# Two more staging places in attention, and the down weights' split moved to behind the third output part, in a fused attention and MoE kernel

## The chip, the cores and the metric

The kernel runs on one core of one Trainium2 chip. The metric is the device time of one execution in microseconds; lower is better. Three runs of the kernel before gave 858.66, 855.82 and 859.16 us, median 858.66. A separate profiled execution gave the trace from which all rows here come.

## The reference

```python
def reference(**kwargs):
    # kernelised attention, 4 batches x 8 heads x 576 tokens x 64
    proj = einsum('bhsd,df->bhsf', x, w_phi); proj -= max(abs(proj), -1)
    phi = concatenate([exp(proj), exp(-proj)], -1)
    attn = (phi(q) @ (phi(k).T @ v)) / (phi(q) @ sum(phi(k)) + 1e-6)
    x = attn.reshape(2304, 512)
    # dense gated MLP, 512 -> 1536 -> 512
    g = x @ w_gate
    x = (g / (1 + exp(-g)) * (x @ w_val)) @ w_out
    # top-1 mixture, 8 experts, 512 -> 1024 -> 512
    e = argmax(x @ gate); out = prob[e] * sigmoid(x @ output_gate)[e] * relu(x @ w1[e]) @ w2[e]
```

All inputs are fp32 (this is a shortened form; the softmax of the gate and the mask by expert are left out).

## The kernel before, in words

**Attention** takes the span up to about 155 us: 16 units (two heads each), with the order of the instructions of all engines written down in `PLAN_TABLE`. Beside it the MLP's weights are brought into the resident tiles `WR[f][0..2]` (f is one of 12 slices of the hidden width; [0] and [1] are gate and value, [2] is the down weight, called W2 below). Ten of the 36 tiles are brought in later, one to a block, by `conv_late` (L447 and L456 on ACT, L464 and L468 on DVE, L472 on POOL). The transposed attention output of the token blocks behind the first two leaves through a staging place: `x_keep` (ACT, L415) copies a piece of PSUM to `XS[i]`, `x_store` (L419) sends it to DRAM, and the place is free when the transfer has landed. There are two places, `TS` and `GP`.

**The MLP** is computed for three pairs of token blocks, p = 0, 1, 2, of 768 tokens each. Every fp32 operand is split in two fp32r parts, hi and lo: `cut` copies hi on ACT (L551) and subtracts it from the source for lo (L548) on DVE or POOL. A product is then three matmuls, hi*hi, hi*lo, lo*hi (L591 to L593, and L494 to L496). Gate and value are made for both token blocks at once from seven products instead of eight, so that sums of weights (`weight_sum`, four per slice, L560, POOL) and sums of the two halves of the input stand in for plain operands. `pair(p)` runs 12 blocks f. In program order a block issues on PE

A11 (6 matmuls), O0 (3), A12 (6), S2 (6), O1 (3), first half of S3 (3), S1 (6), second half of S3 (3), O2 (3), S4 (6), A22 (6),

where O0, O1, O2 (`o_part`) are the down projection of the slice two blocks back, for three tiles of tokens, with the split W2. Below, s is the start of the last matmul of S1 in a block. The other engines' parts of a block:

- `copy` (L619, ACT) takes PSUM to SBUF: `sp1` behind A11, `su2` behind S2, `su4` behind S1.
- `gate` is a tanh (L622, ACT) and an elementwise operation (L623, DVE) from PSUM.
- `add` (L616, DVE): `add(pa, su4, py)` behind S3, on which A22 waits, since A22 goes on in the bank `py`; `add(hb, gb, pa)` at the end, on which the next block's A12 waits, since it starts in the bank of `pa`.
- three splits for the next block: `pair_split(3f+3)` of a plain weight, lo on POOL, and behind it the four weight sums of a later slice; `pair_split(3f+4)` and `pair_split(3f+5)` of weight sums, lo on DVE. They are called the first, second and third split here. The first two weight sums write over what the second split reads, the other two over what the third reads.
- the split of W2 for the next block's O0 (lo on POOL, 128x512), and `cut22`, the split for A22 (lo on POOL, 128x256).
- one step of `rest`, the small operations of the routing of earlier tokens (L883), in p = 1 and 2.

`down(p)` follows each pair: 12 iterations of 9 matmuls project the kept second halves (`hb`), with their splits issued two iterations ahead, and two more groups of three tiles with W2 at iterations 0 and 2. From iteration 3 on, `fill` pops one entry of a list (`post`: three logits steps with L924 and L925, then L932 and L934, L939 and L940, then routing). In the last `down`, 2 MB weight loads of the first expert run beside it.

What decides the order: in attention the table; behind it Tile's scheduler, by its own estimate, under the data dependences and under `tie`, a dependence of the schedule alone (no semaphore) on the matmul in `state["pe"]`. Each engine then runs its own instructions in that order.

Of the kernel before, what the change touches and what calls it, by code (L numbers as in the profile page):

```python
# [53 lines left out]
class Arena:  # L54
# [10 lines left out]

PLAN_LOG = None
PLAN_TABLE = [
# [34 lines left out]


class Plan:
# [84 lines left out]
def kernel(ctx, tc, qT, kT, v1, wphi, w1cat, wlog, mw1, mw2, consts, out):  # L189
# [80 lines left out]
    assert st + 1664 <= ar.p  # L270
    TS = buf(BT)
    GP = buf(BT)
    XS = [TS, GP]
    offs["KR"] = ar.p
    QK = [buf(2 * S) for _ in range(2)]
    V = [buf(VW) for _ in range(2)]
# [212 lines left out]
    def o_tiles(on, last, ts, out_, g, w):  # L489
        (gh, gl), (woh, wol) = g, w  # L490
        for t in ts:
            ps = PS[:, out_[t], :]
            ts_ = slice(t * P, (t + 1) * P)
            PE.matmul(ps, gh[:, ts_], woh, start=not on, stop=False)  # L494
            PE.matmul(ps, gh[:, ts_], wol, start=False, stop=False)
            mm = PE.matmul(ps, gl[:, ts_], woh, start=False, stop=last)  # L496
        return mm
# [50 lines left out]
        eng.tensor_tensor(out=w[1], in0=src, in1=w[0].bitcast(F32), op=ALU.subtract)  # L548

    def cut(w, src, eng):  # L550
        ACT.activation(w[0], src, AF.Copy)  # L551
        cut_lo(w, src, eng)

    def weight_sum(f, i, eng=None):
# [58 lines left out]
    def pair(p, rest):  # L613

        def add(out_, x, y, op=ALU.add):
            DVE.tensor_tensor(out=out_, in0=x, in1=y, op=op)  # L616
# [17 lines left out]
        def o_part(f, ts):  # L634
            g = f - 2
            if g >= 0:
                o_tiles(g != 0, False, ts, bk["O"], (GH[g % 2], GL[g % 2]), W2)

        for f in range(p == 0, NFT):
            sp1, su2, su4, gb = TMP  # L640
            bb = BB[f % 2]
            pb = PS[:, bb, :BT]
            product(p, f, "A11", bb, True)
            copy(sp1, pb)
            o_part(f, (0,))
            hidden(f - 1)
            product(p, f, "A12", BA, True)
            add(pa, sp1, pa)
            product(p, f, "S2", bb, False)
            copy(su2, pb)  # L650
            gate(GP, pa)
            pair_split(48 * p + 3 * f + 3)
            o_part(f, (1,))
            product(p, f, "S3", BY, True, (0,))
            rest(p, f, 0)
            product(p, f, "S1", bb, False)
            copy(su4, pb)
            if f == NFT - 1:
                cut(g5(p, 0), hb(p, stretch(p)[0]), DVE)
            pair_split(48 * p + 3 * f + 4)  # L660
            product(p, f, "S3", BY, True, (1,))
            add(pa, su4, py)
            o_part(f, (2,))
            rest(p, f, 1)
            product(p, f, "S4", bb, False)
            gate(gb, pb)
            if f == NFT - 1:
                cut(g5(p, 1), hb(p, stretch(p)[1]), DVE)
            pair_split(48 * p + 3 * f + 5)
            product(p, f, "A22", BY, False)  # L670
            add(hb(p, f), gb, pa, ALU.mult)
            if p < NP - 1:
                SP.dma_start(out=hd[p][f], in_=hb(p, f))
            add(py, su2, py)
            add(py, GP, py, ALU.mult)
            cut22(f + 1)
            if f:
                cut(W2, WR[f - 1][2], POOL)
            rest(p, f, 2)
        hidden(NFT - 1)  # L680

    def first_part():
# [13 lines left out]
        def unit(u, d0):  # L696
# [23 lines left out]
            for part in range(2):  # L720
                h = op("PE", 36 - 12 * part, lambda b, part=part: tx_mm(u, part, b), [("xt", 0), ("xt2", 1)] if part == 0 else
                       [("xt2", 0), ("xt", 1)], [("txm", u, part)], 1, due=d0 + 17)
                for x in x_pieces(u, part):
                    j, w = x[1], 17 + x[3] * 8 // 100
                    if j < 2:
                        op("ACT", w, lambda b, x=x: x_copy(u, x, b, ACT), [("txm", u, part)], [("xf", j, u)], holder=h, due=d0 + 17,
                           alt=("DVE", w, lambda b, x=x: x_copy(u, x, b, DVE)))
                        continue
                    i = len(kept) % 2
                    kept.append(x)  # L730
                    op("ACT", w, lambda b, x=x, i=i: x_keep(u, x, b, i), [("txm", u, part)], [("xs", i)], holder=h, due=d0 + 17)
                    op("SP", 30, lambda x=x, i=i: x_store(u, x, i), [("queue",), ("xs", i)], [("xdma", len(kept))], due=d0 + 18)
# [703 lines left out]
    def down(p):  # L1436
# [8 lines left out]
        for i, f in enumerate(order_):  # L1445
# [4 lines left out]
                pair_split(48 * p + 39 + i)  # L1450
            if not end and i + 4 < NFT:
                SP.dma_start(out=HS3[order_[i + 4] % 4], in_=hd[p][order_[i + 4]])
            mm = o_tiles(i > 0, i == NFT - 1, range(3), bk["O2"], g5(p, i), w)
            state["pe"] = mm.ins
            if end and 2 <= i < 6:
                gather_q(0, [i - 2])
            if i == 0:
                o_tiles(True, False, range(3), bk["O"], (GH[0], GL[0]), W2)
                cut(W2, WR[NFT - 1][2], POOL)
            if i == 1 and end:  # L1460
                load_w(0, 1)
# [1 line left out]
            if i == 2:  # L1463
                o_tiles(True, True, range(3), bk["O"], (GH[1], GL[1]), W2)
                for t in range(3):
                    post_x2(n - 1, t)
            if i >= 3 and (end or i < 8):
                fill(1)
            if not end:
                if i >= 3 and xs:  # L1470
# [21 lines left out]
    for i in range(2):  # L1492
        load_w(1, i)
    state["banks"] = [7]
    todo += [(idle, ())] * 3 + post(5) + route_late()
    quads(fill)
    ch = Chunks()
    moe2(NQ, NQ + NSS, ch)
# [51 lines left out]
```

## Time and profile before

| what | value |
|---|---|
| median of three runs | 858.66 us (855.82 to 859.16) |
| profiled execution | 858.48 us, its span 856.7 us |
| granted clock of TensorE, mean | 0.995 |
| busy PE, DVE, ACT, POOL | 97%, 70%, 59%, 52% of the span |
| stages (start, us) | attention 0, block f=0 of p=0 155.6, down 277, p=1 311, down 425, p=2 458, down 574, experts 612.5 |

PE's busy time counts matmuls whose ends are modelled, so 97% says only that it seldom stands still. A row of the timeline has the start, the duration, engine and line, the operation and, in brackets, how long the engine was idle before it and what released it.

### The profile page before, as it was taken

The numbers are of one execution on the slowest core, as the hardware profiler recorded it, in microseconds if no ns is written. First come the engines' busy times: TensorE is split into PE (matmuls) and PEld (weight loads), VectorE is DVE, ScalarE is ACT, GpSimd is POOL, SyncE is SP. The second block draws the span as 40 slices with busy tenths as digits, with TensorE's granted clock in tenths as the row PEclk, the third lists the DMA queues.
The fourth block names the chain that finished last, engine by engine and source line by source line (L and its number), as shares of the span: only waits on it lengthen the run. The fifth ranks groups of instructions, "written<-read, shape, count | busy, mean of one in ns | idle before, by whom it ended". The sixth has DMA issues, their size and how long they took to land. (4 is left out here: it accounts for less than half of the span.)

```text
span 856.7 us, 17319 instructions
## 1 busy us (share of the span) xinstructions
PE 827.2 (97%) x6701; PEld 723.2 (84%) x6701; DVE 595.6 (70%) x1106; ACT 504.9 (59%) x938; POOL 443.9 (52%) x414
## 2 busy tenths in 40 slices
PE   8999999899999999999999999998999999999995
PEld 5999899798889789999978899996778888888884
DVE  6999899777777668666776777774686434445692
ACT  5787888566666566546656565563434434344883
POOL 2877889777677556556655566446202111120120
PEclk9999999999999999999999999999999999999998
DMA  9676784412222230000121000019402331010650
GB/s 253 193 227 169 237 246 153 135 53 79 78 69 71 93 111 28 19 19 20 56 83 37 2 1 1 2 27 388 151 1 63 136 124 73 24 51 0 248 212 11
DMA packets 30875, 84.57 MB, mean 99 GB/s; under 512 B 6462, under 2 KB 15678, under 8 KB 29504
## 3 DMA queue, kind: packets, MB, share of 16 engines
q1 hardware_dynamic: 27216, 73.57, 26.7%
q0 software_dynamic: 3200, 9.48, 3.4%
q8 instruction: 54, 0.88, 0.5%
q10 hardware_dynamic: 368, 0.33, 0.2%
q14 instruction: 37, 0.30, 0.1%
HBM read 79.13 MB, written 17.86 MB: 113 GB/s over the span
## 5 line engine op out<-in xcount | busy, mean ns | idle before, releaser
L551 ACT ACTIVATE r_dense<-arena 128x512 fp32r<-128x512 f32 (+1 forms) x150 | 92.8, 622 | 102.2 <-PE banks L592 70.7
L560 POOL TENSOR_TENSOR arena<-arena 128x256 f32<-128x256 f32 x140 | 103.9, 753 | 90.7 <-DVE r_dense L548 87.6
L548 POOL TENSOR_TENSOR r_dense<-arena,r_dense 128x512 fp32r<-128x512 f32 x73 | 97.7, 1339 | 42.2 <-ACT r_dense L551 36.5
L591 PE MATMUL banks<-arena_r,r_dense 128*128 128x384 f32 x288 | 98.1, 343 | 3.5 <-ACT arena L415 1.9
L1215 ACT ACTIVATE arena_r<-arena 128x512 fp32r<-128x512 f32 x64 | 40.3, 633 | 102.1 <-PE banks L1226 49.2
L548 DVE TENSOR_TENSOR r_dense<-arena,r_dense 128x512 fp32r<-128x512 f32 (+1 forms) x83 | 70.2, 846 | 43.2 <-ACT r_dense L551 20.8
L1218 DVE TENSOR_TENSOR arena_r<-arena,arena_r 128x512 fp32r<-128x512 f32 x64 | 44.4, 694 | 79.7 <-ACT arena_r L1215 78.5
L593 PE MATMUL banks<-arena_r,r_dense 128*128 128x384 f32 x288 | 97.0, 337 | 0.0
L592 PE MATMUL banks<-arena_r,r_dense 128*128 128x384 f32 x288 | 96.8, 336 | 0.0
L616 DVE TENSOR_TENSOR banks<-arena,banks 128x384 f32<-128x384 f32 x140 | 77.8, 556 | 12.6 <-PE banks L593 9.8
L1176 POOL DMA_INDIRECT out_dram<-arena x20 | 24.1, 1204 | 106.1 <-ACT arena L1270 41.0
L1171 POOL DMA_INDIRECT ov_gather<-x2d,arena x20 | 21.0, 1048 | 100.4 <-PE banks L1185 54.8
L591 PEld LDWEIGHTS banks<-arena_r,r_dense 128*128 128x128 f32 x288 | 53.9, 188 | 15.4 <-ACT arena L619 2.7
L619 ACT ACTIVATE arena<-banks 128x384 f32<-128x384 f32 x105 | 50.7, 484 | 25.0 <-PE banks L593 23.2
L623 DVE SCALAR_TENSOR_TENSOR arena<-arena,banks 128x384 f32<-128x384 f32 x70 | 38.7, 553 | 35.1 <-ACT arena L622 34.9
L548 POOL TENSOR_TENSOR arena_r<-arena,arena_r 128x512 fp32r<-128x512 f32 x36 | 47.5, 1321 | 21.5 <-ACT arena_r L551 21.5
L592 PEld LDWEIGHTS banks<-arena_r,r_dense 128*128 128x128 f32 x288 | 54.1, 188 | 2.0
L593 PEld LDWEIGHTS banks<-arena_r,r_dense 128*128 128x128 f32 x288 | 54.1, 188 | 0.1
L332 DVE TENSOR_REDUCE arena<-banks 128x6 f32<-128x768 f32 x48 | 45.8, 955 | 9.5 <-PE banks L326 6.8
L591 PE MATMUL banks<-ov_pair,r_dense 128*128 128x384 f32 x144 | 49.7, 345 | 1.3 <-ACT arena L619 0.9
L1225 PE MATMUL banks<-arena_r 128*128 128x512 f32 x128 | 50.4, 393 | 0.0
L1226 PE MATMUL banks<-arena_r 128*128 128x512 f32 x128 | 49.9, 390 | 0.0
(217 smaller groups left out, 2376.0 us busy)
## 6 DMA issues: line engine op xcount, KB each, us to landing
arena<-mw SPq DMA_DIRECT2D x16, 2048.0 KB, 8.7
ov_conv<-w1cat SPq DMA_DIRECT2D x18, 512.0 KB, 6.1
arena<-w1cat SPq DMA_DIRECT2D x18, 512.0 KB, 3.5
arena<-v SPq DMA_DIRECT2D x16, 325.0 KB, 3.8
hd<-arena SPq DMA_DIRECT2D x24, 192.0 KB, 1.8
x2d<-arena SPq DMA_DIRECT2D x18, 256.0 KB, 3.9
arena<-qT SPq DMA_DIRECT2D x15, 288.0 KB, 4.3
arena<-kT SPq DMA_DIRECT2D x15, 288.0 KB, 6.8
```

Source lines behind the costliest of these rows:

```text
L332: DVE.tensor_reduce(out=MX, in_=ps, axis=AX.X, op=ALU.max, apply_absolute_value=True)
L548: eng.tensor_tensor(out=w[1], in0=src, in1=w[0].bitcast(F32), op=ALU.subtract)
L551: ACT.activation(w[0], src, AF.Copy)
L560: (eng or POOL).tensor_tensor(out=o, in0=x, in1=y, op=op)
L591: PE.matmul(ps, w[0][:, c], xh[:, k, :], start=(start and k == 0), stop=False, skip_group_check=True)
L592: PE.matmul(ps, w[0][:, c], xl[:, k, :], start=False, stop=False, skip_group_check=True)
L593: state["pe"] = PE.matmul(ps, w[1][:, c], xh[:, k, :], start=False, stop=(k == 1), skip_group_check=True).ins
L616: DVE.tensor_tensor(out=out_, in0=x, in1=y, op=op)
L619: ACT.activation(out_, x, AF.Copy)
L1218: DVE.tensor_tensor(out=l, in0=src, in1=h.bitcast(F32), op=ALU.subtract)
L1225: PE.matmul(ps, wh[:, c], XQH[:, k, :], start=(k == 0), stop=False)
L1226: PE.matmul(ps, wh[:, c], XQL[:, k, :], start=False, stop=False)
```

## The change

The change has six parts. (1) `x_keep` has four staging places instead of two; the two new ones are the first 384 columns of the W2 tiles of slices 10 and 11, which are brought in later. (2) The table of attention's order is a new one. (3) The hi copy of every `cut` is tied to the last matmul in `state["pe"]`, which `o_part` now sets too. (4) In a block the second split stands behind the second half of S3 and `add(pa, su4, py)`, no more ahead of them. (5) The split of W2 stands right behind O2, no more at the end of the block. (6) In `down`, iteration 0 computes two tiles of its own, then the three tiles with W2, then its third tile; `fill` runs at iterations 5 to 11 of the last `down` (before 3 to 11), and 4 to 8 of the others (before 3 to 7); and one idle entry of the list is taken out before the last token block's steps.

```diff
 PLAN_TABLE = [
-    0, 2, 4, 5, 6, 1, 3, 14, 15, 16, 531, 538, 29, 17, 18, 21, 532, 30, 31, 7, 19, 43, 45, 47, 22, 32, 10, 20, 33, 539,
+    0, 1, 14, 15, 2, 3, 5, 16, 17, 4, 18, 538, 29, 531, 21, 19, 532, 30, 6, 7, 8, 1534, 31, 539, 32, 43, 22, 45, 44, 20,
...
-    XS = [TS, GP]
+    XS = [TS, GP] + [WR[NFT - 2 + i][2][:, 0:BT] for i in range(2)]
...
     def cut(w, src, eng):
-        ACT.activation(w[0], src, AF.Copy)
+        a = ACT.activation(w[0], src, AF.Copy)
+        if "pe" in state:
+            tie(a)
         cut_lo(w, src, eng)
...
         def o_part(f, ts):
             g = f - 2
             if g >= 0:
-                o_tiles(g != 0, False, ts, bk["O"], (GH[g % 2], GL[g % 2]), W2)
+                state["pe"] = o_tiles(g != 0, False, ts, bk["O"], (GH[g % 2], GL[g % 2]), W2).ins
...
                 cut(g5(p, 0), hb(p, stretch(p)[0]), DVE)
-            pair_split(48 * p + 3 * f + 4)
             product(p, f, "S3", BY, True, (1,))
             add(pa, su4, py)
+            pair_split(48 * p + 3 * f + 4)
             o_part(f, (2,))
+            if f:
+                cut(W2, WR[f - 1][2], POOL)
             rest(p, f, 1)
...
             cut22(f + 1)
-            if f:
-                cut(W2, WR[f - 1][2], POOL)
             rest(p, f, 2)
...
-                    i = len(kept) % 2
+                    i = len(kept) % 4
...
-            mm = o_tiles(i > 0, i == NFT - 1, range(3), bk["O2"], g5(p, i), w)
+            if i == 0:
+                o_tiles(False, False, (0, 1), bk["O2"], g5(p, i), w)
+                o_tiles(True, False, range(3), bk["O"], (GH[0], GL[0]), W2)
+            mm = o_tiles(i > 0, i == NFT - 1, range(3) if i else (2,), bk["O2"], g5(p, i), w)
             state["pe"] = mm.ins
...
             if i == 0:
-                o_tiles(True, False, range(3), bk["O"], (GH[0], GL[0]), W2)
                 cut(W2, WR[NFT - 1][2], POOL)
...
-            if i >= 3 and (end or i < 8):
+            if i >= 5 if end else 4 <= i < 9:
                 fill(1)
...
-    todo += [(idle, ())] * 3 + post(5) + route_late()
+    todo += [(idle, ())] * 2 + post(5) + route_late()
```

On DVE, a middle block of p = 1. L616 to `r_dense` is the lo part of the hidden slice; the L548 are the second and third split; L623 the two gates; of the L616 to `banks`, the second is `add(pa, su4, py)`. Before:

```order
L616 TENSOR_TENSOR r_dense<-banks,r_dense 128x384
L616 TENSOR_TENSOR banks<-arena,banks 128x384
L548 TENSOR_TENSOR r_dense<-arena,r_dense 128x512
L623 SCALAR_TENSOR_TENSOR arena<-arena,banks 128x384
L548 TENSOR_TENSOR r_dense<-arena,r_dense 128x512
L616 TENSOR_TENSOR banks<-arena,banks 128x384
L883 TENSOR_TENSOR arena<-arena,banks 128x24
L623 SCALAR_TENSOR_TENSOR arena<-arena,banks 128x384
L616 TENSOR_TENSOR banks<-arena,banks 128x384
L616 TENSOR_TENSOR arena<-arena,banks 128x384
```

The same block with the change (L616 is now L618, L623 is L625):

```order
L618 TENSOR_TENSOR r_dense<-banks,r_dense 128x384
L618 TENSOR_TENSOR banks<-arena,banks 128x384
L625 SCALAR_TENSOR_TENSOR arena<-arena,banks 128x384
L618 TENSOR_TENSOR banks<-arena,banks 128x384
L548 TENSOR_TENSOR r_dense<-arena,r_dense 128x512 x2
L625 SCALAR_TENSOR_TENSOR arena<-arena,banks 128x384
L618 TENSOR_TENSOR banks<-arena,banks 128x384
L618 TENSOR_TENSOR arena<-arena,banks 128x384
L618 TENSOR_TENSOR banks<-arena,banks 128x384
```

Both splits have moved behind `add(pa, su4, py)`, and stand together ahead of the second gate.

On POOL, a middle block of p = 1: to `arena_r` is the lo part of W2, to `r_dense` that of the first split, to `arena_r_63` that of `cut22`, L560 the weight sums. Before:

```order
L560 TENSOR_TENSOR arena<-arena 128x256 x4
L548 TENSOR_TENSOR arena_r<-arena,arena_r 128x512
L548 TENSOR_TENSOR r_dense<-arena,r_dense 128x512
L548 TENSOR_TENSOR arena_r_63<-arena,ov_pair 128x256
L560 TENSOR_TENSOR arena<-arena 128x256 x4
```

With the change (L560 is now L562):

```order
L548 TENSOR_TENSOR r_dense<-arena,r_dense 128x512
L562 TENSOR_TENSOR arena<-arena 128x256
L548 TENSOR_TENSOR arena_r<-arena,arena_r 128x512
L562 TENSOR_TENSOR arena<-arena 128x256 x3
L548 TENSOR_TENSOR arena_r_63<-arena,ov_pair 128x256
```

The lo part of W2 has moved from behind all four sums to behind the first of them.

On POOL, late blocks of p = 0, where L472 is the last step of `conv_late`. Before:

```order
L560 TENSOR_TENSOR arena<-arena 128x256 x2
L472 TENSOR_TENSOR arena<-arena 128x512
L560 TENSOR_TENSOR arena<-arena 128x256 x2
L548 TENSOR_TENSOR arena_r<-arena,arena_r 128x512
L548 TENSOR_TENSOR r_dense<-arena,r_dense 128x512
L548 TENSOR_TENSOR arena_r_63<-arena,ov_pair 128x256
```

With the change:

```order
L548 TENSOR_TENSOR r_dense<-arena,r_dense 128x512
L472 TENSOR_TENSOR arena<-arena 128x512
L548 TENSOR_TENSOR arena_r<-arena,arena_r 128x512
L562 TENSOR_TENSOR arena<-arena 128x256 x4
L548 TENSOR_TENSOR arena_r_63<-arena,ov_pair 128x256
```

Here L472 and the lo part of W2 now stand next to each other, ahead of all four sums.

## Rows read from the trace of the kernel before

**Rows 1.** The page's busy time by engine: busy us, share of the span, instructions.

```profile
PE 827.2 (97%) x6701; PEld 723.2 (84%) x6701; DVE 595.6 (70%) x1106; ACT 504.9 (59%) x938; POOL 443.9 (52%) x414
```

**Rows 2.** Busy time by stretch (PE, PEld, DVE, ACT, POOL, clock, DMA): the blocks of p = 0 and of p = 1.

```profile
169.50:277.00 107.50, 104.05 (x547) 95.19 (x547) 83.35 (x131) 70.17 (x139) 79.91 (x86) 1.00 0.22 71
...
311.40:425.00 113.60, 112.79 (x631) 105.75 (x630) 76.17 (x165) 67.04 (x139) 71.24 (x81) 1.00 0.12 39
```

**Rows 3.** PE's waits: line, what released it, total us, times, longest us.

```profile
PE banks L591 <- DVE banks L616: 3.2, 8, 0.4
PE banks L924 <- DVE arena L925: 2.4, 1, 2.4
...
PE banks L591 <- ACT arena L415: 1.9, 2, 1.0
PE banks L591 <- ACT arena L619: 1.7, 2, 0.9
...
PE banks L494 <- DVE arena L616: 0.8, 1, 0.8
```

**Rows 4.** Timeline of ACT at the start of p = 0.

```profile
157.94 0.33 ACT L415 ACTIVATE arena<-banks 128x192 f32<-128x192 f32 x1 [2.57 <-DMA xd<-arena]
...
162.72 0.66 ACT L456 ACTIVATE arena<-arena 128x512 int32<-128x512 uint32 x1 [1.39 <-DMA arena<-w1cat]
```

**Rows 5.** Timeline of one block of p = 0: DVE, POOL, then PE.

```profile
203.46 1.57 DVE L548 TENSOR_TENSOR r_dense<-arena,r_dense 128x512 fp32r<-128x512 f32 x1 [0.35 <-PE banks L593]
...
203.18 1.29 POOL L472 TENSOR_TENSOR arena<-arena 128x512 int32<-128x512 int32 x1 [0.71 <-DVE arena L468]
...
205.55 0.44 PE L591 MATMUL banks<-arena_r,ov_pair 128*128 128x384 f32 x1 [0.41 <-DVE banks L616]
```

**Rows 6.** Timeline of one block of p = 1: PE, ACT, DVE, then POOL.

```profile
393.39 0.33 PE L593 MATMUL banks<-ov_pair,r_dense 128*128 128x384 f32 x1
...
394.55 0.40 PE L496 MATMUL banks<-arena_r,r_dense 128*128 128x512 f32 x1
...
398.60 0.34 PE L591 MATMUL banks<-arena_r,r_dense 128*128 128x384 f32 x1
...
394.13 0.47 ACT L619 ACTIVATE arena<-banks 128x384 f32<-128x384 f32 x1
395.04 0.63 ACT L551 ACTIVATE arena_r<-arena 128x512 fp32r<-128x512 f32 x1 [0.44 <-PE banks L496]
...
396.89 0.56 DVE L623 SCALAR_TENSOR_TENSOR arena<-arena,banks 128x384 f32<-128x384 f32 x1 [1.02 <-ACT arena L622]
...
397.83 0.55 DVE L616 TENSOR_TENSOR arena<-arena,banks 128x384 f32<-128x384 f32 x1
...
395.02 1.46 POOL L560 TENSOR_TENSOR arena<-arena 128x256 f32<-128x256 f32 x2 [1.70 <-DVE r_dense L548]
```

**Rows 7.** Timelines of DVE and POOL where both work, at 268 and 326 us.

```profile
269.43 2.16 DVE L548 TENSOR_TENSOR arena_r<-arena,arena_r 128x384 fp32r<-128x384 f32 x2
...
268.86 1.30 POOL L548 TENSOR_TENSOR r_dense<-arena,r_dense 128x512 fp32r<-128x512 f32 x1
270.11 1.05 POOL L548 TENSOR_TENSOR arena_r<-arena,ov_pair 128x256 fp32r<-128x256 f32 x1
...
326.14 0.48 DVE L883 TENSOR_TENSOR arena<-arena 128x24 f32<-128x24 f32 x1
326.54 0.68 DVE L548 TENSOR_TENSOR r_dense<-arena,r_dense 128x512 fp32r<-128x512 f32 x1
...
325.83 3.37 POOL L560 TENSOR_TENSOR arena<-arena 128x256 f32<-128x256 f32 x4 [2.90 <-DVE r_dense L548]
```

**Rows 8.** The last down: timeline of DVE, then busy time of two stretches.

```profile
593.08 0.69 DVE L925 COPY arena<-banks 128x512 f32<-128x512 f32 x1 [1.99 <-DMA x2d<-arena]
...
595.00:597.00 2.00, 2.00 (x10) 1.10 (x12) 0.96 (x2) 0.39 (x1) 0.00 (x0) 0.52 1.06 447
597.00:599.00 2.00, 2.00 (x11) 0.68 (x12) 1.05 (x2) 0.72 (x2) 1.20 (x1) 0.63 1.01 419
```

66 rows, old and new, of the table PLAN_TABLE are left out of this document.

## The prediction

> **What bounds it now.** I read the busy time by engine first: PE 97%, DVE 70%, ACT 59%, POOL 52% [rows 1]. So the kernel is bound by PE, and what a change of order can give back is the time in which PE stands still, or runs at the lower clock. By stretch, PE is idle 3.45 of 107.5 us in p = 0 and only 0.8 of 113.6 us in p = 1 [rows 2]: there is something to win in p = 0, and nearly nothing in p = 1 and p = 2, where the change can only cost. The list of PE's waits names the places [rows 3]: eight waits on an `add` of DVE (3.2 us), one of 2.4 us on the logits' copy L925, two on `x_keep` (1.9), two on the copies L619 (1.7), one of 0.8 us at the start of a `down`. The timelines of these places then give the causes.
>
> **How DVE and POOL get in each other's way.** This decides most of the sum. In p = 0, POOL's L472 ran from 203.18 to 204.47; DVE's split, which takes 0.68 us alone [rows 7], began at 203.46 and ended at 205.03, so 0.56 us behind POOL's end [rows 5]. It did nothing while POOL's operation lasted. Two rules follow, and I price by them: an operation of DVE with two SBUF inputs waits for the end of a POOL operation that was there first, and then needs 0.56 us; and one of DVE that already waits goes ahead of POOL's next. For the second: at 326 us a small DVE operation waited out POOL's first sum, ended at 326.62, and DVE's split ran in 0.68 us directly behind it, while POOL's four sums took 3.37 us [rows 7], where two take 1.46 [rows 6]. At 268.86 the turns alternated: POOL, DVE, POOL (1.05 us for a 128x256 split), DVE, the two DVE splits taking 2.16 us [rows 7].
>
> The Trainium skill (SBUF — State Buffer, section "SBUF: two separate sides") says that the pair of ports which the two share is held for a whole instruction by whichever starts first; the trace agrees on that (0.56 us behind POOL's end, above). It says nothing of who is next when both wait.
>
> **The sum, part by part** (profiled execution 858.48 us, which is its span of 856.7 and 1.8 around it; 0.2 below the median).
>
> *Attention, four places.* ACT stood idle 2.57 us ahead of an `x_keep` until a transfer had landed [rows 4], and PE then waited 1.9 us in two places [rows 3]; each wait also costs a slow restart. With two more places this goes. But the 1.39 us that ACT waited for a load of weights [rows 4] stays, and the order of all of attention is new. Best case 5, worst 0; I take -3.0. The two new places lie in tiles that are brought in late in p = 0, when their stores have long landed, so they cost nothing themselves; SP issues the same transfers.
>
> *p = 0.* The third split now stands behind `add(pa, su4, py)`, so the eight waits ahead of A22 go: 3.2 us and 0.11 each for the restart (0.44 against 0.33 us) [rows 5, 6], together -4.2. In their place: L472 and then the lo part of W2 stand on POOL just when DVE wants both splits. From s (the start of S1's last matmul) L472 ends at about s+2.0 to 2.3. The second split then ends at s+2.6 to 2.9; W2's lo part, 1.15 to 1.29 us like the POOL operations of its shape [rows 5, 7], holds POOL until s+3.8 to 4.1; the third split ends at s+4.3 to 4.6. Behind it stand the gate and the `add` to `hb`. Now the gate starts 3.50 and `hb` ends 4.99 behind s, and the next A12, which waits for `hb`, starts 5.21 behind s [rows 6]: 0.2 us to spare, and the gate 0.8 to 1.1 late. That is a new wait of 0.6 to 0.9 ahead of A12; 0.8 in nine blocks is +7.2. Together **+3.0** (0 to +5).
>
> *The ties* are no semaphores, so they cost only through the order that results, which is priced here by block.
>
> *p = 1 and 2, the clean block.* `su4` can start at about s+0.4 and takes 0.47 [rows 6]; activations overlap by 0.1; the second split's hi, 0.63, ends at s+1.4 and its lo part at s+2.1. POOL's first sum waits for that and takes 0.73 (half of 1.46): it ends at about s+2.93. W2's hi part follows O2's last matmul by 0.49, at s+1.65 [rows 6], and the third split's hi by the tie behind it: it ends at s+2.80. The lo part of the third split asks at s+2.83, so 0.1 us before the sum ends. By the second rule it goes ahead of W2's lo part, ends at s+3.6, and `hb` at s+5.1: no wait. W2's lo part then ends at s+4.8 to 4.9, where O0 needs it about half a us ahead of A12, so at s+4.74: 0.08 in some 18 blocks, +1.5.
>
> *p = 1 and 2, blocks in which DVE is late.* In f = 1 of both, the lo part of W2 stands ahead of all sums: +0.4 each, +0.8. In five more the third split cannot ask before s+2.93: two have an exp of the routing ahead of its hi part on ACT, one has two logits copies of 0.69 [rows 8] ahead of it on DVE, one a reciprocal behind a small operation that had to wait, one a 128x384 product. There W2's lo part goes first, 1.15 to 1.29, and `hb` is late by some 1.05: **+5.2**. In five others a small operation with two SBUF inputs waits out the sum directly ahead of the split; as at 326 us it costs nothing, as at 268 us 1.1: half, +2.7. Both waits on L619 were there before [rows 3]; the earlier `su4` takes some of them: -1.0.
>
> *Downs.* The 0.8 us wait [rows 3] and its restart go, since the tiles with W2 now stand ahead of the third tile: -1.0. In the last one PE waited 2.4 us for L925 [rows 3], which waited for the store of x2 to land, behind the 2 MB loads (DVE at 593.08) [rows 8]. Two iterations later the store has landed: -2.5, and 0.3 for a smaller wait behind it. PE also fell to the lower clock after standing still, 0.52 of full speed in 595 to 597 and 0.63 in 597 to 599 [rows 8]; 48% and 37% of 2 us are 1.7 us: -1.7. The steps that no longer fit go into the experts' start: +0.5. Together **-5.0** (-7 to 0).
>
> -3.0 + 3.0 + 1.5 + 0.8 + 5.2 + 2.7 - 1.0 - 5.0 = +4.2. Laid on the median of 858.66, which is 0.2 above the profiled execution, that is 862.9: **863 us**. 0.5%, about what a measurement of this kernel can tell from no change, is 4.3 us, so this lies at the edge of slower.
>
> **Rivals.**
>
> *The port is no trouble (faster).* If DVE also gets its turn where I have it lose, and L472 in p = 0 is done earlier, the +5.2, +2.7, +1.5 and half of the +7.2 go: 863 - 13 = 850 us. For it: at 326 us DVE kept the port over two operations. Against it: 203.46. It is decided by whether the third split asks before the first sum ends.
>
> *DVE loses in every block (slower).* The margin in the clean block is 0.1 us out of sums of eight durations. If POOL's next operation takes the port at the sum's end, `hb` is 1.0 late in another 13 blocks or so: 863 + 13 = 876 us. For it: POOL's instructions follow each other without a gap. Against it: 326.54. By the page's words the pair is free between two instructions of POOL, which speaks for DVE's turn; no rule there gives it to POOL.
>
> *The last down keeps its wait.* The loads go on beyond 599 us at a full DMA share, 1.06 and 1.01 [rows 8], so a later logits step may meet them too, and PE's waits stay in attention because of the load of weights: 863 + 4 = 867 us.
>
> **How the numbers follow.** My forecast 0.45, spread around the bound (0.25 slower, 0.15 within 0.5%, and 0.05 faster, if attention gives its full 5 and the unsure collisions nothing); port no trouble 0.30 (0.25 faster, 0.05 within); DVE always late 0.12; the last down keeps its wait 0.13 (0.10 slower, 0.03 within). So faster 0.30, same 0.23, slower 0.47. The forecast's own range is 855 to 869; with the rivals, leaving out a tenth on each side, 848 to 877.
>
> **What will show it.** Right: no waits of PE on L618 ahead of A22 in p = 0, but waits ahead of A12 there on L618 to `hb`, of 0.5 to 0.9 us in most blocks; in p = 1 and 2 such waits of about 1 us in five to ten blocks and none in the clean ones; no wait on the logits' copy and a full clock in the last down; `x_keep` not held by its store. Wrong: waits ahead of A12 in nearly all blocks (the second rival) or nearly none (the first), or PE still idle in attention's last 10 us.

## The result, and the profile after

The changed kernel took 866.27 us (median of four runs, 866.07 to 867.5) against 857.52 for the kernel before in the same comparison (four runs, 855.82 to 859.16): ratio 1.0105, 95% interval 1.008 to 1.0131, so about 1% slower. The profiled execution's span grew from 856.7 to 865.7 us. The prediction was 863, slower, with a range of 848 to 877.

The page's busy time by engine, after:

```profile
PE 829.9 (96%) x6701; PEld 725.2 (84%) x6702; DVE 621.4 (72%) x1103; ACT 498.1 (58%) x937; POOL 467.8 (54%) x418
```

PE does the same 6701 matmuls in nearly the same time. DVE is busy 25.8 us longer than in [rows 1], with three instructions fewer, and POOL 23.9 us longer, with four more. Those four are operations of attention, some 8 us of work; most of the rest is none, since an operation that waits for the other engine counts as busy. DVE's splits show it, before and after (the second number behind the bar is the mean in ns):

```profile
L548 DVE TENSOR_TENSOR r_dense<-arena,r_dense 128x512 fp32r<-128x512 f32 x71 | 59.0, 832 | 31.5 <-PE banks L593 20.6 <-ACT r_dense L551 9.1 <-ACT r_dense L794 1.8
L548 DVE TENSOR_TENSOR r_dense<-arena,r_dense 128x512 fp32r<-128x512 f32 x72 | 80.3, 1119 | 10.2 <-ACT r_dense L551 10.0
```

The list of PE's waits, after (line, what released it, total us, times, longest us; L593 to L595 are the product's matmuls, L618 is `add`, L832 and L835 are the same steps of ACT and DVE in block 0):

```profile
PE banks L593 <- DVE arena L618: 11.8, 19, 0.8
PE banks L593 <- DVE banks L835: 1.7, 1, 1.7
...
PE banks L593 <- ACT arena L621: 1.2, 2, 0.6
...
PE banks L387 <- issue: 1.1, 1, 1.1
PE banks L593 <- ACT arena L832: 0.9, 1, 0.9
PE banks L357 <- issue: 0.9, 2, 0.7
...
PE banks L495 <- POOL arena_r L548: 0.2, 1, 0.2
```

Against [rows 3], the eight waits of 3.2 us ahead of A22 (`add` to `banks`) are gone, and so are those on L925 and on `x_keep` in the blocks. In their place stand nineteen waits of 11.8 us on `add` to `arena`: that is `hb`, on which A12 waits. In block 0 of p = 0 the wait on L835 grew from 0.3 to 1.7 us, that on L832 from 0.4 to 0.9.

Where the time went, from the start of the first matmul of each stage:

| stage | before, us | after, us | difference |
|---|---|---|---|
| attention, to block 0 of p = 0 | 155.59 | 158.48 | +2.89 |
| p = 0, blocks 0 and 1 | 21.96 | 21.06 | -0.90 |
| p = 0, blocks 2 to 10 | 90.28 | 92.35 | +2.07 |
| block 11 and the first down | 43.58 | 42.80 | -0.78 |
| p = 1, block 0 | 8.81 | 9.60 | +0.79 |
| p = 1, blocks 1 to 10 | 95.50 | 100.55 | +5.05 |
| block 11 and the second down | 42.67 | 41.75 | -0.92 |
| p = 2, blocks 0 to 10 | 105.56 | 109.27 | +3.71 |
| block 11, the last down, the experts | 292.75 | 289.84 | -2.91 |

Timeline of one block of p = 0 after (compare [rows 5]): DVE, POOL, PE.

```profile
207.88 3.14 DVE L548 TENSOR_TENSOR r_dense<-arena,r_dense 128x512 fp32r<-128x512 f32 x2
210.94 0.54 DVE L625 SCALAR_TENSOR_TENSOR arena<-arena,banks 128x384 f32<-128x384 f32 x1
...
211.87 0.54 DVE L618 TENSOR_TENSOR arena<-arena,banks 128x384 f32<-128x384 f32 x1
...
207.47 1.30 POOL L472 TENSOR_TENSOR arena<-arena 128x512 int32<-128x512 int32 x1 [2.04 <-DVE arena L468]
208.81 1.66 POOL L548 TENSOR_TENSOR arena_r<-arena,arena_r 128x512 fp32r<-128x512 f32 x1
...
212.47 0.44 PE L593 MATMUL banks<-arena_r,r_dense 128*128 128x384 f32 x1 [0.63 <-DVE arena L618]
```

The chain that was forecast can be read off. POOL's L472 ends at 208.77; DVE's second split waited for it. W2's lo part then holds POOL until 210.47, and the third split, the second of the two in the first row, ends at 211.02, 0.55 behind it. The gate follows at 210.94, `hb` ends at 212.41, and A12 starts at 212.47 after 0.63 us of nothing.

Two blocks of p = 1 after, first one without a wait, then one with:

```profile
350.67 0.69 DVE L548 TENSOR_TENSOR r_dense<-arena,r_dense 128x512 fp32r<-128x512 f32 x1 [0.45 <-ACT r_dense L551]
...
350.02 0.74 POOL L562 TENSOR_TENSOR arena<-arena 128x256 f32<-128x256 f32 x1 [2.98 <-DVE arena L885]
350.72 1.80 POOL L548 TENSOR_TENSOR arena_r<-arena,arena_r 128x512 fp32r<-128x512 f32 x1
```

```profile
392.02 0.83 DVE L885 TENSOR_TENSOR arena<-arena 128x24 f32<-128x24 f32 x2
392.78 1.78 DVE L548 TENSOR_TENSOR r_dense<-arena,r_dense 128x512 fp32r<-128x512 f32 x1
...
391.98 0.74 POOL L562 TENSOR_TENSOR arena<-arena 128x256 f32<-128x256 f32 x1 [2.79 <-DVE r_dense L548]
392.68 1.33 POOL L548 TENSOR_TENSOR arena_r<-arena,arena_r 128x512 fp32r<-128x512 f32 x1
...
396.00 0.45 PE L593 MATMUL banks<-arena_r,r_dense 128*128 128x384 f32 x1 [0.82 <-DVE arena L618]
```

In the first, the third split asks at 350.67, while the sum runs to 350.76, and goes next; W2's lo part takes 1.80 in place of 1.30, since it waits. In the second, two small operations of the routing waited out the sum, the split came 0.1 us behind POOL's next, and took 1.78.

### The profile page after: what moved, and what is told of

The parts are those of the page before. It is cut to its first block, busy times and chain, and to the rows that moved or that the text cites. A ratio compares the mean times of both kernels' runs of the same rounds, so it can differ in the third digit from the quotient of the medians.

```text
span 865.7 us, 17185 instructions
## 1 busy us (share of the span) xinstructions
PE 829.9 (96%) x6701; PEld 725.2 (84%) x6702; DVE 621.4 (72%) x1103; ACT 498.1 (58%) x937; POOL 467.8 (54%) x418
## 4 chain that ended last, share of the span: by engine, by line
PE 71%; DVE 17%; issue 5%; ACT 2%; DMA 2%; POOL 2%; DVEq 0%; POOLq 0%; SPq 0%; ACTq 0%
PE banks L593 7%; PE banks L595 6%; PE banks L594 6%; PE banks L495 4%; PE banks L494 4%; PE banks L496 4%; DVE r_dense L548 4%; PE banks L1227 3%; PE banks L1229 3%; PE banks L1243 3%; PE banks L1241 3%; PE banks L1242 3%; PE banks L1228 3%; PE banks L387 3%; PE banks L326 3%
## 5 line engine op out<-in xcount | busy, mean ns | idle before, releaser
L562 POOL TENSOR_TENSOR arena<-arena 128x256 f32<-128x256 f32 x140 | 109.9, 803 | 68.3 <-DVE r_dense L548 36.3
L548 POOL TENSOR_TENSOR r_dense<-arena,r_dense 128x512 fp32r<-128x512 f32 x72 | 99.8, 1389 | 40.1 <-ACT r_dense L551 39.7
L593 PE MATMUL banks<-arena_r,r_dense 128*128 128x384 f32 x288 | 100.5, 349 | 13.6 <-DVE arena L618 11.8
L618 DVE TENSOR_TENSOR banks<-arena,banks 128x384 f32<-128x384 f32 x140 | 77.7, 555 | 32.8 <-ACT arena L621 24.7
L548 DVE TENSOR_TENSOR r_dense<-arena,r_dense 128x512 fp32r<-128x512 f32 (+1 forms) x84 | 89.5, 1069 | 13.5 <-ACT r_dense L551 13.3
L595 PE MATMUL banks<-arena_r,r_dense 128*128 128x384 f32 x288 | 97.4, 339 | 0.7 <-POOL r_dense L548 0.7
L594 PE MATMUL banks<-arena_r,r_dense 128*128 128x384 f32 x288 | 97.3, 338 | 0.0
L593 PEld LDWEIGHTS banks<-arena_r,r_dense 128*128 128x128 f32 x288 | 54.2, 188 | 28.2 <-DVE arena L618 20.5
L548 POOL TENSOR_TENSOR arena_r<-arena,arena_r 128x512 fp32r<-128x512 f32 x36 | 54.8, 1521 | 15.7 <-ACT arena_r L551 15.3
L625 DVE SCALAR_TENSOR_TENSOR arena<-arena,banks 128x384 f32<-128x384 f32 x70 | 38.4, 549 | 27.2 <-ACT arena L624 27.0
L472 POOL TENSOR_TENSOR arena<-arena 128x512 int32<-128x512 int32 x29 | 37.8, 1308 | 32.5 <-DVE arena L468 32.3
L595 PEld LDWEIGHTS banks<-arena_r,r_dense 128*128 128x128 f32 x288 | 54.4, 189 | 1.0 <-POOL r_dense L548 1.0
L593 PE MATMUL banks<-ov_pair,r_dense 128*128 128x384 f32 x144 | 49.7, 345 | 1.2 <-ACT arena L621 1.2
L1227 PE MATMUL banks<-arena_r 128*128 128x512 f32 x128 | 50.4, 393 | 0.0
```

What stands on the lines that cost most here:

```text
L562: (eng or POOL).tensor_tensor(out=o, in0=x, in1=y, op=op)
L593: PE.matmul(ps, w[0][:, c], xh[:, k, :], start=(start and k == 0), stop=False, skip_group_check=True)
L594: PE.matmul(ps, w[0][:, c], xl[:, k, :], start=False, stop=False, skip_group_check=True)
L595: state["pe"] = PE.matmul(ps, w[1][:, c], xh[:, k, :], start=False, stop=(k == 1), skip_group_check=True).ins
L1227: PE.matmul(ps, wh[:, c], XQH[:, k, :], start=(k == 0), stop=False)
```

## The experiments

All ratios are against the kernel before, run in the same comparison.

**W2's split back at the end of the block** (e3).

```diff
             o_part(f, (2,))
-            if f:
-                cut(W2, WR[f - 1][2], POOL)
             rest(p, f, 1)
...
             cut22(f + 1)
+            if f:
+                cut(W2, WR[f - 1][2], POOL)
```

> The change with W2's split back at the end of the block. DVE's order stays exactly that of the change; W2's parts move behind the gate on ACT and behind the four sums on POOL. Theory (W2's lo part is what DVE's third split waits for): PE's waits on L618 ahead of A12 go, 11.8 us now, under 2 us then; but W2's lo part ends later than O0 wants it, a new wait of L495 on POOL of 1 to 2 us in about 20 blocks: 866 to 885 us. Rival (the second gate is late because both splits stand ahead of it on DVE, whatever POOL does): the waits on L618 stay at 8 to 12 us.

Measured: 941.82 us, ratio 1.1004 (1.0962 to 1.1045). Its waits, and a block of p = 0 on POOL, then on DVE:

```profile
PE banks L495 <- POOL arena_r L548: 60.6, 32, 3.1
```

```profile
199.01 1.30 POOL L472 TENSOR_TENSOR arena<-arena 128x512 int32<-128x512 int32 x1 [4.90 <-DVE arena L468]
200.93 3.33 POOL L562 TENSOR_TENSOR arena<-arena 128x256 f32<-128x256 f32 x4 [0.63 <-DVE r_dense L548]
204.22 0.72 POOL L548 TENSOR_TENSOR arena_r<-arena,ov_pair 128x256 fp32r<-128x256 f32 x1
204.90 1.26 POOL L548 TENSOR_TENSOR arena_r<-arena,arena_r 128x512 fp32r<-128x512 f32 x1
```

```profile
200.01 1.44 DVE L548 TENSOR_TENSOR r_dense<-arena,r_dense 128x512 fp32r<-128x512 f32 x2
201.76 0.56 DVE L625 SCALAR_TENSOR_TENSOR arena<-arena,banks 128x384 f32<-128x384 f32 x1 [0.30 <-ACT arena L624]
```

No wait on L618 is left, with DVE's order untouched. The list alone does not decide it, since the new wait stands ahead of A12 and would cover one on `hb`. The timeline of DVE (above, the same block) does: both splits run in 1.44 us, and the gate starts behind its tanh on ACT (L624), not behind the split. In blocks 2 to 10 of p = 0 `hb` ends 4.5 to 5.1 us behind s, where the change has 6.0 to 6.1, and A12 would start at s+5.2 if it waited for nothing. So POOL's lo part of W2 is what the third split waited for; the rival falls. The size of the new wait was missed by far: it is some 2 us in 32 blocks, and the mean clock fell to 0.966. Once the two later splits stand late in the block, the four sums, which write over what they read, move late too, and W2's lo part behind them ends long after O0 wants it. The place behind O2 is what makes the other edits of the block bearable at all; which of the two, the ties or the second split's place, needs it more was not run.

**The third split behind the last elementwise steps** (e7), all else as changed.

```diff
-            pair_split(48 * p + 3 * f + 5)
             product(p, f, "A22", BY, False)
...
             add(py, GP, py, ALU.mult)
+            pair_split(48 * p + 3 * f + 5)
             cut22(f + 1)
```

> The change with the third split moved behind the last elementwise steps of the block; W2's split stays behind O2. Theory (the second gate and hb are late because they queue behind the third split, which waits for W2's lo part on POOL): PE's 19 waits on L618 ahead of A12 (11.8 us and a restart of some 0.15 each) go: 850 to 854 us. Rival (the tie, and W2's lo part on POOL in the middle of the block, hold up the gate by themselves): 862 to 867 with the waits left.

Measured: 851.24 us, ratio 0.9937 (0.9918 to 0.9956). No wait on L618 is among its largest:

```profile
PE banks L595 <- POOL r_dense L548: 2.7, 3, 1.5
PE banks L326 <- issue: 1.3, 1, 1.3
```

Blocks 2 to 10 of p = 0 are 4.32 us shorter than before, so 6.4 shorter than with the change, and those of p = 1 and 2 lose 3.4 and 3.8 us of what they had grown by. With W2's split and the ties where the change put them, moving one split on DVE gave back 15 us, 13.6 us of the profiled span in these stretches. (On POOL, two of the four sums moved with it, behind `cut22`, since they write over what the third split reads.) The wait was in the order on DVE, and the theory holds on both sides.

**Attention as before, the rest as changed** (e1).

```diff
-    XS = [TS, GP] + [WR[NFT - 2 + i][2][:, 0:BT] for i in range(2)]
+    XS = [TS, GP]
...
-                    i = len(kept) % 4
+                    i = len(kept) % 2
```

and the old table.

> The change with attention as before: two staging places and the old table, all else as changed. Theory (in the trace block f=1 of p=0 starts 2.6 us later with the change, so the new order of attention costs 2.6): 863.7 us, 862.5 to 865. Rival (the late start of the blocks is taken up later, the whole loss is made in the blocks): 866, 865.5 to 867.

Measured: 866.37 us, ratio 1.0111 (1.0085 to 1.0138): the rival. Block 0 starts at 155.50, 3.0 us earlier than with the change, but block 1 takes 10.57 us in place of 8.92, with waits on `x_keep` again, and the profiled spans differ by 1.0 us (864.7 and 865.7). Its list:

```profile
PE banks L593 <- DVE arena L618: 11.8, 19, 0.8
PE banks L593 <- ACT arena L621: 1.6, 2, 1.0
...
PE banks L593 <- ACT arena L415: 0.9, 1, 0.9
```

The nineteen waits stand unchanged, so they do not hang on attention.

**Four places, every instruction in the old order** (e2), on the kernel before: the planner goes on with two places in its books, and the copies and stores use four.

```diff
-                    i = len(kept) % 2
+                    i, q = len(kept) % 2, len(kept) % 4
...
-                    op("ACT", w, lambda b, x=x, i=i: x_keep(u, x, b, i), [("txm", u, part)], [("xs", i)], holder=h, due=d0 + 17)
+                    op("ACT", w, lambda b, x=x, q=q: x_keep(u, x, b, q), [("txm", u, part)], [("xs", i)], holder=h, due=d0 + 17)
```

> The kernel before with four staging places in fact, but every instruction in the old order. Theory (the waits of x_keep for its store, and PE's 1.9 us behind them, go; the loss in attention comes from the new order): 2 to 4 us faster than before, 853.5 to 856. Rival (the load of weights that ACT also waits for holds the blocks anyway): within 1 us of before.

Measured: 854.16 us, ratio 0.9977 (0.9958 to 0.9996): 2.1 us faster. Blocks 0 and 1 of p = 0 are 3.1 us shorter, and no wait on L415 is among the largest. The places do what the prediction had them do.

**The edits of the downs alone** (e4), and **of `fill` alone** (e14), on the kernel before.

```diff
-            if i >= 3 and (end or i < 8):
+            if i >= 5 if end else 4 <= i < 9:
...
-    todo += [(idle, ())] * 3 + post(5) + route_late()
+    todo += [(idle, ())] * 2 + post(5) + route_late()
```

e4 also has the change's order of the tiles at iteration 0.

> The kernel before with the change's edits of the downs alone: the order of the tiles at iteration 0, fill two iterations later, one idle entry less. Theory (the trace of the change ends 2.9 us earlier from the last pair's last block on, and is 0.8 and 0.9 us shorter in the other two downs; no logits copy is waited for in the last down, and no fall of the clock): 4 to 5 us faster than before, 851 to 853. Rival (the downs are shorter only since the pairs ahead of them end later): 0 to 2 us faster.

> The kernel before with the edit of fill and the idle entry alone; the tiles of the downs in the old order. Theory (PE's 2.4 us wait for the logits copy, which waits for a store to land, and the fall of the clock behind it are what the later fill takes away): the wait on L925 at L924 gone, 2 to 4 us faster than before, 853 to 855. Rival (the later steps meet the weight loads too, so a new wait): 857 to 858.

Measured: e4 853.23 us, ratio 0.9954 (0.9935 to 0.9974); e14 853.86 us, 0.9959 (0.9946 to 0.9973). So nearly all of it is `fill`; what the tiles' order adds is inside the intervals. Timeline of PE in e14's last down, the three logits steps, and its busy time and clock around them (compare [rows 8]):

```profile
592.38 0.60 PE L924 MATMUL banks<-arena 128*128 128x128 f32 x4
594.90 0.60 PE L924 MATMUL banks<-arena 128*128 128x128 f32 x4
597.41 0.60 PE L924 MATMUL banks<-arena 128*128 128x128 f32 x4
```

```profile
591.00:595.00 4.00, 4.00 (x21) 3.26 (x20) 1.74 (x1) 1.83 (x5) 3.78 (x4) 1.00 1.08 382
595.00:599.00 4.00, 4.00 (x26) 3.43 (x25) 3.66 (x5) 2.48 (x5) 2.87 (x3) 1.00 1.02 430
```

PE does not stand still in these 8 us, and the clock stays at 1.00 where it had been 0.52 and 0.63.

**The third split late and tied, on the kernel before** (e10). Only this split is tied; no run here has it late without the tie.

```diff
-    def cut(w, src, eng):
-        ACT.activation(w[0], src, AF.Copy)
+    def cut(w, src, eng, tied=False):
+        a = ACT.activation(w[0], src, AF.Copy)
+        if tied:
+            tie(a)
...
-            cut(slot(i), SPR[f % 2][w - 1], DVE)
+            cut(slot(i), SPR[f % 2][w - 1], DVE, w == 2 and "pe" in state)
```

and the move of e7.

> The kernel before with one edit: the third split stands behind the last elementwise steps of the block and is tied there; nothing else is tied, W2's split stays where it was. Theory (in p = 0 DVE's third split, held by L472, delays add(pa, su4, py) and with it A22): the eight waits ahead of A22 go, 8 times 0.57: 3.5 to 5 us faster than before, 851 to 853. Rival (A22 waits for the sum of S3 and su4 anyway): no change.

Measured: 849.24 us, ratio 0.9915 (0.9888 to 0.9943). The direction is the theory's, the 8 us are more than it asked for. By stage (the profiled span is 10.2 us shorter), blocks 0 and 1 of p = 0 give 1.3, blocks 2 to 10 give 5.5 and those of p = 2 1.3; 2.0 lie in the last down and the experts, where nothing was changed. That stage also came out 2.4 us shorter in e2, which touches attention alone. The traces show why: in both, PE's wait on the logits' copy in the last down took 1.7 us where it had been 2.4, and the clock did not fall behind it. In e10, whose L926 and L927 are the logits step L924 and its copy L925 (wait, then busy time and clock behind it):

```profile
PE banks L926 <- DVE arena L927: 1.7, 1, 1.7
```

```profile
587.00:591.00 4.00, 4.00 (x27) 2.70 (x26) 1.10 (x3) 1.83 (x4) 1.29 (x1) 1.00 1.01 422
```

So some 2 us in this stage differ between profiled executions without an edit there.

**Combinations.** e9 is e7 with attention in the old order and four places; e12 is e10 with four places in the old order and the edits of the downs; e13 is e12 with the change's new order of attention.

> The change with the third split behind the last elementwise steps, and attention in the old order with four places. Theory (the new order of attention starts the blocks 1 to 3 us later, and with the waits in the blocks gone this shows): 1 to 3 us under the kernel with the third split late alone, 848 to 850. Rival (the blocks' first waits take it up again, as with the change): 851.

> The kernel before with the late, tied third split, four places in the old order, and the edits of the downs, without the change's ties and without its place for W2's split. Theory (the three gains are in different stages and add up: 2 and 4 and 4.6): 844 to 847 us. Rival (they take the same slack in part): 848 to 851.

> The fastest kernel so far (late tied third split, the edits of the downs, four places in the old order; 844.6 us) with the change's new order of attention in place of the old. Theory (the blocks start 1 to 3 us later with it, and nothing in these blocks takes that up): 846 to 848 us. Rival (the first blocks take it up, as they did in the change): 844 to 845.

Measured: e9 847.72 us, ratio 0.9893 (0.9868 to 0.9918), 3.5 us under e7; of the 4.5 us between the two profiled spans, 1.6 lie ahead of block 0 and 2.6 in blocks 0 and 1 of p = 0. e12 **844.64 us, ratio 0.9859** (0.9831 to 0.9886), the fastest of all: the three gains (2.1, 8.0 and 4.0) nearly add up, to 12.6 us, without the ties of every split and with W2's split in its old place. What is left in its list behind attention is small, first:

```profile
PE banks L934 <- DVE arena L927: 1.1, 2, 0.6
...
PE banks L593 <- ACT arena L832: 0.9, 1, 0.9
```

e13 took 851.39 us, ratio 0.9937 (0.9924 to 0.995), worse than either theory. Its attention ends no later than e12's; one wait in block 1 of p = 0 makes the difference (PE, then POOL, then busy time and clock behind it):

```profile
173.25 0.69 PE L595 MATMUL banks<-arena_r,r_dense 128*128 128x384 f32 x1 [6.01 <-POOL r_dense L548]
...
167.06 2.22 POOL L562 TENSOR_TENSOR arena<-arena 128x256 f32<-128x256 f32 x3
169.24 1.26 POOL L548 TENSOR_TENSOR r_dense<-arena,r_dense 128x512 fp32r<-128x512 f32 x1
170.58 1.40 POOL L562 TENSOR_TENSOR arena<-arena 128x256 f32<-128x256 f32 x2
171.94 1.26 POOL L548 TENSOR_TENSOR r_dense<-arena,r_dense 128x512 fp32r<-128x512 f32 x1
```

```profile
174.00:178.00 4.00, 4.00 (x14) 4.00 (x14) 0.18 (x1) 0.44 (x1) 0.00 (x0) 0.51 0.00 0
```

A split that PE wants stands behind five weight sums and another split on POOL, and PE ran at the lower clock behind the wait. So the new order of attention does not end later here; it meets the blocks' first instructions badly, by 6 us of waiting and some 2 of lower clock (an estimate: 13 matmuls 0.32 us apart, which are 0.17 apart at the full clock).

## Why the prediction was right, and where it was not

That the time fell into the range says little: the measured difference of 8.75 us is twice the 4.2 that were forecast, and the range had room for a faster kernel too. What carries the forecast is its account by stage. One term, attention, missed by 5 us; the sums of the other stages came within 1 us.

**What bounds it** held: PE's matmuls took nearly the same time, and what changed is when PE stands still.

**p = 0, +3.0.** Right in both halves. The eight waits ahead of A22 went, and nine waits ahead of A12 came, 0.79 to 0.92 us each from matmul to matmul, where 0.8 had been put in. Blocks 2 to 10 grew by 2.07. The -4.2 for the waits ahead of A22 (its own figures give 4.1) was too small: e10, which takes them away and brings none, shortens these blocks by 5.5.

**p = 1 and 2, the clean block.** Right that DVE goes first when it asks before the sum ends, by less than 0.1 us at 350.67. The +1.5 for W2's lo part was not there: it ended at 352.52, and only one wait of 0.2 on it is listed.

**p = 1 and 2, late blocks, +8.7 together.** The sum was right, the places half: ten waits ahead of A12, 0.42 to 0.99, together 8.0. The blocks with f = 1 lost nothing. Of the five in which a small operation with two SBUF inputs stands directly ahead of the split, counted at half, four lost their turn.

**Earlier `su4`, -1.0.** Wrong sign: block 0 of p = 1 grew by 0.79, p = 2's shrank by 0.14.

**Downs, -5.0.** Measured -0.78, -0.92 and -2.91 by stage, together -4.6, and 4.0 us in the medians of e4. The wait on L925 went and the last down keeps its full clock; e14 shows both without the rest. Two things the sum did not have. Two waits ahead of L932, one in each of the first two downs, stand in no term of it, and they are gone as well (before):

```profile
PE banks L932 <- DVE arena L925: 2.3, 2, 1.2
```

And the 1.7 us for the clock were won in the last down but not over the whole execution: in the profiled execution of the change PE ran at the lower clock in blocks 0 and 1 of p = 0, where it waited 0.9 and 1.7 us (L832 and L835 above).

```profile
168.80:172.20 3.40, 3.03 (x9) 3.03 (x10) 1.44 (x4) 0.42 (x1) 3.32 (x5) 0.51 0.03 8
```

The mean granted clock was 0.995 before and 0.994 after. The profiled executions of e1, e4 and e14 have such a stretch there too; those of e2, e7, e9, e10 and e12 have none ahead of their last 10 us. In e2 and e10 the clock stayed at 1.00 behind a wait of 1.7 us in the last down, so the fall there was no fixed price of that wait.

**Attention, -3.0: the term that failed.** Through block 1 of p = 0 the change was 2.0 us later than before, not 3.0 earlier. The mechanism of the places was right (e2: -2.1), but the prediction took the new order of everything else in attention to be free. In the change, attention as before or new gives the same median (e1). In the profiled execution, block 0 starts 2.9 us later, and 2.5 of PE's time in attention went in waits for which the profile names no releaser ("issue": L387 1.1 and L357 0.9, listed above, and one of 0.5). Blocks 0 and 1 then won 0.9, where e2 wins 3.1: in them stand the longer wait on L835, now 1.7 us, and the lower clock, some 1.3 us (an estimate: nine matmuls 0.32 us apart, which are 0.17 apart at the full clock). That the new order has a price is shown by e9 against e7 (3.5 us) and e13 against e12 (6.8). With this term at +2 in place of -3 the sum would have been +9.2 instead of +4.2; the spans differ by 9.0.

What stays open: what the issue waits are. With the same order of attention, block 0 started at 158.48, 157.23, 156.38 and 155.61 in four kernels (the change, e7, e3, e13), so they are not fixed by the order alone. With the old order it started at 155.3 to 155.7 in seven, but at 157.27 in e14, which has 0.6 us of issue waits. How much of the 2.9 us is the new order's is therefore not shown.

## What to carry to other kernels

Read which operations of DVE and POOL stand next to each other in time, and what queues behind the one that loses: here a split that nobody needed for half a block delayed, by about 1 us in most blocks of p = 0, the gate and the `add` that PE was waiting for. Putting work with slack behind the work that PE waits for (one move with one tie, e10) was worth 8 us by itself, where the six parts of the change together lost 9. When an edit gets its value only together with another (the change's ties and its place for the second split need W2's split behind O2, and without it cost 75 us more), time the parts against the kernel before, not only against each other.

## What the runs showed of the hardware that I had not expected

At 326 us a DVE split followed a small operation with no turn for POOL in between [rows 7]; at 392.78 POOL's next operation came in between, and the split took 1.78 us. What decided was which of the two began first. In 15 blocks of p = 1 and 2 of the changed kernel the third split and W2's lo part were ready at nearly the same time. In eight the split began at s+2.83 to 2.88, 0.02 to 0.05 us ahead of W2's part; it took 0.69 us and W2's part 1.8. In seven it began at s+2.92 or later, behind W2's part at s+2.88 or 2.89, and took 1.66 to 1.81 us. A small operation directly ahead did not keep the turn for the split by itself: it did in one of five blocks. And the wait for a turn shows as busy time: DVE's 26 us more are hardly work, and of POOL's 24 some 8 are.
